# Identity products that go on into the second batch of a linear-attention and three-gate maxout kernel

## The chip, the cores and the metric

One core of one Trainium2 chip runs the whole problem. The metric is the device time of one execution in microseconds (us). Four engines compute: TensorE (PE in the rows; PEld is its weight load), VectorE (DVE), ScalarE (ACT) and GpSimd (POOL). SyncE's queue (SPq) issues the DMAs.

## The reference

There are 8 batches of 8 heads, 576 positions and a head dimension of 64. The attention's output, 4608 tokens of 512 features, goes through a layer of three gates and one output matrix.

```python
q_s = exp(q - max(q, -1)); q_s = q_s / (sum(q_s, -1) + 1e-09)
k_s = exp(k - max(k, axis=2)); k_s = k_s / (sum(k_s, axis=2) + 1e-09)
kv = einsum('bhsd,bhse->bhde', k_s, v)
x = einsum('bhsd,bhde->bhse', q_s, kv)        # as rows of 512
h = maximum(maximum(x @ w1, x @ w2), x @ w3)  # 512 to 768
return h @ w_out                              # 768 to 512
```

## The kernel before

The program is written out in full: no loop runs on the chip. Work is cut into steps, and a planner in the kernel's own Python (`Streams`) puts the steps of each engine in order. It keeps one clock for each engine (`self.clock["T"]` is TensorE's), adds a cost for each step, and issues next the step that may begin first. The costs only decide the order; on the chip, semaphores decide when something runs. What the planner thinks idle and what is idle on the chip are therefore two things.

Heads are taken in pairs, four pairs to a batch. A pair of batch 0 or 1 goes through these lines. `kt` is exponentiated (L692, ACT) and turned by four transposes into a `pa` bank (L698) and a fifth into the small bank (L699). ACT or DVE copies both to `ke` (L703 from `pa`, L704 from the small bank). The product of keys and values goes into the small bank (L773, 20 rows on PE), and ACT scales it into `bdf` (L783). The queries are turned (L899) and copied to `qf` (L903, ACT or DVE). L941 multiplies `qf` by `bdf`; ACT takes the high word of the result (L944), for some pairs PE subtracts it (L947), and ACT or DVE takes the low word (L949 or L952). The gates (L1052) multiply these words by the words of the weights `wa`, three products to a step, twelve to a gate. Slices of the weights are loaded and split at the same time (L546, L555 to L584).

The small bank is one PSUM bank of 512 columns, of which a pair has columns 128 to 255 for L699 and L704, 256 to 383 for L773 and L783; one pair (pair 1) has columns 384 to 511 for sums. Columns 0 to 127 are used by nothing. Batch 0 takes its small banks from the pool `pf` of four. Batch 1 (pairs 4 to 7) takes them from the pool `sm`, which has one bank, so that pair after pair has the same bank.

Before batch 1 takes it, that bank belongs to a tile `spare`. Into it go products of the identity with itself (L509), 128 columns of float32, each of which is two MATMUL rows in the trace; nothing reads them. `Streams.issue` calls `fill` with the hole that the planner sees ahead of a TensorE step, as long as TensorE's planned clock is under `SPARE[2]`:

```python
if e == "T" and SPARE[0] < t and self.clock["T"] < SPARE[2]:
    self.fill(max(self.clock["T"], SPARE[0]), t)
```

`fill` gives 0.65 of the hole to products of 0.225 us each, and writes them ahead of the step. By `self.taken.get("sm")` it stops once a pair of batch 1 has the bank.

Tiles are handed out by pools, and the framework writes the semaphores. It orders the accesses of different engines to one PSUM bank as whole accesses to that bank, whatever their columns: an access waits for those that stand ahead of it in the order of the program.

Of the kernel before, what the change touches and what calls it, by code (L numbers as in the profile page):

```python
# [8 lines left out]
F32 = mybir.dt.float32  # L9
# [22 lines left out]

COLD = 11.5, 1.85

SPARE = 4.4, 11.5, 42.0, 0.65

FIRST, CHUNK, SLICE = 144.74, 26.23, 2.59

# [160 lines left out]
class Streams:  # L199
# [100 lines left out]
    def fill(self, a, b):  # L300

        n = int((min(b, SPARE[1]) - a) / (0.225 * COLD[1])) if a < SPARE[1] else 0
        a = max(a, SPARE[1])
        n += int((b - a) * SPARE[3] / 0.225) if b > a else 0
        if n > 0 and not self.taken.get("sm"):
            self.spare(n)

    def issue(self, t, e, c, s):
        step = s[4]
        if e == "T" and t < COLD[0]:  # L310
            c *= COLD[1]
        if e == "T" and SPARE[0] < t and self.clock["T"] < SPARE[2]:
            self.fill(max(self.clock["T"], SPARE[0]), t)
        end = t + c
# [26 lines left out]
def linear_attention_then_maxout_ffn(  # L341
# [27 lines left out]
    nc = tc.nc  # L369
    B, H, S, D = 8, 8, 576, 64  # L370
    DM, DF = 512, 768
    P = 128
# [4 lines left out]
    CH = 512  # L377
# [40 lines left out]
    sm = ctx.enter_context(tc.tile_pool(name="sm", bufs=BANKS[1], space=PSUM))  # L418
    dram = ctx.enter_context(tc.tile_pool(name="dram", bufs=1, space=bass.MemoryType.DRAM))
    start_stack = ExitStack()  # L420
    start = start_stack.enter_context(tc.tile_pool(name="start", bufs=2, side="right"))
# [28 lines left out]
    ident = const.tile([P, P], F32, name="ident")  # L450
# [29 lines left out]
    for i in range(0, P, BL):  # L480
        nc.vector.tensor_scalar(
            out=ident[i : i + BL, :], in0=count[i : i + BL, :], scalar1=turned_count[i : i + BL, i : i + 1],
# [19 lines left out]
    for c in range(PAIRED, B + 1, 2):  # L502
        in_pf += [("S", c, i) for i in range(4)] + [(c, "y", t) for t in range(8)]
    st = Streams({"pf": 4, "pa": BANKS[0], "sm": BANKS[1], "hp": NJ, "tmp": 3, "ke": 2, "kep": 1, "qe": 2, "qf": 1, "qt": 1, "tb": 1, "qT": 1, "qhl": 1, "xr": 1, "ws": len(ws), "hs": 3}, {"pf": in_pf, "hs": in_hs, "ws": in_ws, "tb": list(range(TURNED * NP, B * NP, 2))})
    spare = sm.tile([P, CH], F32, name="sm")

    def products_for_nothing(n):
        for i in range(n):
            nc.tensor.matmul(out=spare[:, 0:P], lhsT=ident, rhs=ident, start=True, stop=True)  # L509

    st.spare = products_for_nothing
    turn_pools = []
# [91 lines left out]
    class Pair:  # L604
# [30 lines left out]

        def take_small(self):
            self.sm = (pf if self.b == 0 else sm).tile([P, CH], F32, name="pf" if self.b == 0 else "sm")

        def k_load(self):
            if self.b:  # L640
                prev = self.ago("ksub") if self.n >= NP + 2 else None
                if self.turned:
                    yield Step("S", 0.5, [prev], gives=("k", self.n), kb=(128, 2304))
                    nc.sync.dma_start(out=self.kt, in_=k_cols[self.b, self.g])
                elif self.m == 0:
                    yield Step("S", 0.5, [prev, ("ksub", self.n - 1)], gives=("k", self.n), kb=(128, 5120))
                    nc.sync.dma_start(
                        out=kboth.rearrange("p h s d -> p (h s d)"), in_=k_rows[self.b - TURNED, self.g // 2]
                    )
# [923 lines left out]
```

## Time and profile before

| | us |
|---|---|
| three runs | 645.25, 645.35, 646.13 |
| their median | 645.35 |
| the profiled execution | 646.05 |
| its span, first to last instruction | 644.2 |
| PE busy within the span | 629.7 |

The profiled execution is 1.85 us longer than its span, and 0.70 us longer than the median of the runs. Its mean granted TensorE clock is 0.997 of full speed.

### The profile page before, as it was taken

The page shows a single profiled execution, that of the slowest core. Times are in us where ns is not written, and L with a number is a line of the kernel's source. Part 1 is how long each engine was busy: PE and PEld are TensorE (multiplying, and loading weights), DVE is VectorE, ACT ScalarE, POOL GpSimd, SP SyncE. Part 2 cuts the span into 40 slices and gives each one's busy share as a digit, 9 for nine tenths or more (in the row PEclk, how much of TensorE's full clock was granted, in tenths as well). Part 3 has the DMA queues.
Part 4 walks back from the last instruction along what each step waited for, and adds up shares of the span by engine and source line. Part 5 has one row for each costly group of instructions (what it writes and reads, how often), then busy time and mean ns, then how long its engine had stood idle before and what let it go on. Part 6 is the DMA issues. An engine that isn't in the chain of part 4 may idle for free.

```text
span 644.2 us, 9789 instructions
## 1 busy us (share of the span) xinstructions
PE 629.7 (98%) x3460; PEld 506.7 (79%) x3460; DVE 423.1 (66%) x750; ACT 309.7 (48%) x678; POOL 58.0 (9%) x57
## 2 busy tenths in 40 slices
PE   6889999999999999999999999999999999999997
PEld 5757877888777787777877877888887888888886
DVE  8988986498997988988666889342425812243420
ACT  5998374235565655855453674322223622213131
POOL 1343333110010000010010000000000000000000
PEclk9999999999999999999999999999999999999999
DMA  8976476798767568999889534576663136666122
GB/s 330 394 246 253 153 229 242 260 342 270 233 222 268 193 206 249 338 293 351 261 279 301 161 117 139 170 240 192 193 191 114 57 127 195 193 195 195 36 65 66
DMA packets 89169, 137.88 MB, mean 214 GB/s; under 512 B 7200, under 2 KB 54816, under 8 KB 86432
## 3 DMA queue, kind: packets, MB, share of 16 engines
q1 hardware_dynamic: 89040, 137.12, 64.8%
q8 instruction: 28, 0.46, 0.3%
q10 hardware_dynamic: 80, 0.13, 0.1%
q14 instruction: 21, 0.17, 0.1%
HBM read 97.12 MB, written 33.03 MB: 202 GB/s over the span
## 4 chain that ended last, share of the span: by engine, by line
PE 74%; DVE 10%; DMA 9%; ACT 3%; issue 1%; SPq 1%; DVEq 0%; ACTq 0%
PE pf L1276 37%; PE pf L1099 18%; PE pf L1052 14%; DMA wst<-in_w_dram 3%; DMA kt<-in_k_rows_dram 2%; DMA bdf<-keep_w 2%; DVE tb L870 1%; PE pa L746 1%; DVE xb L1209 1%; PE pa L969 1%; DMA qT<-tb 1%; DVE bdf L1165 1%; DMA qt<-in_q_rows_dram 1%; DVE xf L1213 1%; DVE mix L1171 1%
## 5 line engine op out<-in xcount | busy, mean ns | idle before, releaser
L1276 PE MATMUL pf<-xb,ws 128*128 128x512 f32 x1134 | 260.8, 390 | 0.2 <-DVE mm L1305 0.2
L1276 PEld LDWEIGHTS pf<-xb,ws 128*128 128x128 f32 x1134 | 212.0, 188 | 45.3 <-DVE mm L1305 0.7
L1052 PE MATMUL pf<-x,wa 128*128 128x512 f32 x648 | 158.6, 399 | 1.0 <-ACT x L949 0.8
L1052 PEld LDWEIGHTS pf<-x,wa 128*128 128x128 f32 x648 | 120.4, 189 | 30.3 <-issue 1.9
L1305 DVE TENSOR_TENSOR mm<-pf,mm 128x512 f32<-128x512 f32 x36 | 24.8, 690 | 88.7 <-PE pf L1276 88.5
L1099 PE MATMUL pf<-oh,hs 128*128 128x512 f32 x192 | 59.4, 390 | 0.0
L1324 ACT COPY pf<-pf 128x512 f32<-128x512 f32 x27 | 15.4, 572 | 84.5 <-PE pf L1276 84.5
L857 ACT ACTIVATE qt<-qt,qs 128x64 f32<-128x64 f32 x171 | 43.4, 336 | 8.7 <-DVE qs L851 6.2
L1099 PEld LDWEIGHTS pf<-oh,hs 128*128 128x128 f32 x192 | 36.0, 188 | 7.7
L570 POOL TENSOR_TENSOR wx<-wx,wst 128x512 int32<-128x512 int32 x24 | 36.0, 1526 | 62.4 <-issue 22.2
L1118 ACT COPY m<-pf 128x512 f32<-128x512 f32 x31 | 18.1, 585 | 44.4 <-PE pf L1099 30.9
L716 POOL PARTITION_ALL_REDUCE kma<-km x24 | 18.5, 773 | 215.4 <-DVE km L713 165.8
L1099 PE MATMUL pf<-ol,hs 128*128 128x512 f32 x96 | 37.7, 393 | 0.0
L870 DVE STREAM_TRANSPOSE tb<-qt 128x576 f32<-128x576 f32 x24 | 30.2, 1272 | 3.3 <-DMA qT<-tb 2.2
L1317 ACT COPY u<-pf 128x512 f32<-128x512 f32 x27 | 15.8, 586 | 32.0 <-PE pf L1276 32.0
L1099 PE MATMUL pf<-oh,mix 128*128 128x512 f32 x96 | 30.2, 395 | 0.0
L1064 DVE TENSOR_TENSOR m<-pf,m 128x512 f32<-128x512 f32 x36 | 24.6, 683 | 8.0 <-PE pf L1052 8.0
L1099 PE MATMUL pf<-ol,h_h 128*128 128x512 f32 x72 | 28.5, 395 | 0.0
L1099 PE MATMUL pf<-oh,h_l 128*128 128x512 f32 x72 | 28.1, 390 | 0.0
L1099 PE MATMUL pf<-oh,h_h 128*128 128x512 f32 x72 | 28.0, 389 | 0.0
L1364 DVE TENSOR_TENSOR hs<-mm,hs 128x512 fp32r<-128x512 f32 (+1 forms) x32 | 16.9, 552 | 13.5 <-ACT hs L1362 13.5
L1317 ACT COPY s<-pf 128x512 f32<-128x512 f32 x27 | 15.8, 587 | 19.4 <-PE pf L1276 16.8
(165 smaller groups left out, 837.5 us busy)
## 6 DMA issues: line engine op xcount, KB each, us to landing
ws<-keep_s SPq DMA_DIRECT2D x108, 256.0 KB, 3.1
ws<-keep_a SPq DMA_DIRECT2D x81, 256.0 KB, 3.1
wst<-in_w_dram SPq DMA_DIRECT2D x12, 1024.0 KB, 7.8
keep_a<-wa SPq DMA_DIRECT2D x12, 768.0 KB, 6.8
keep_s<-mix SPq DMA_DIRECT2D x9, 1024.0 KB, 6.1
vt<-in_v_rows_dram SPq DMA_DIRECT2D x24, 325.0 KB, 4.8
kt<-in_k_rows_dram SPq DMA_DIRECT2D x12, 640.0 KB, 6.4
qt<-in_q_rows_dram SPq DMA_DIRECT2D x12, 576.0 KB, 4.7
```

The source lines that it names most:

```text
L570: nc.gpsimd.tensor_add(out=x.bitcast(I32)[:, at], in0=x.bitcast(I32)[:, at], in1=low.bitcast(I32)[:, at])
L716: nc.gpsimd.partition_all_reduce(kma, km, P, bass_isa.ReduceOp.max)
L857: nc.scalar.activation(out=rows3[:, s, :], in_=rows3[:, s, :], func=AF.Copy, scale=qs[:, s : s + 1])
L870: nc.vector.transpose(out=tb[:, self.m].rearrange("p e (c s) -> p s e c", s=QS), in_=self.qt.rearrange("p s (e c) -> p s e c", e=2),)
L1052: nc.tensor.matmul(out=ps, lhsT=l[:, cc, js], rhs=r, start=(cc == 0 and t == 0), stop=(cc == NC - 1 and t == 2))
L1064: nc.vector.tensor_max(out=m, in0=self.m.pop((j, i)), in1=m)
L1099: nc.tensor.matmul(out=po, lhsT=l, rhs=r[:, j, :], start=(j == 0 and i == 0), stop=(j == NJ - 1 and i == 2))
L1118: nc.scalar.copy(out=o, in_=po)
L1276: nc.tensor.matmul(out=bank[on], lhsT=w[:, k, a], rhs=x[:, b, k], start=(i == 0 and p in ("P1", "P5")), stop=(i == 5), skip_group_check=True,)
L1305: nc.vector.tensor_max(out=m, in0=bank[on], in1=m)
L1317: nc.scalar.copy(out=f, in_=bank[on])
L1364: nc.vector.tensor_tensor(out=o[:, 1, jj], in0=mm[:, h, jj, ts], in1=o[:, 0, jj].bitcast(F32), op=ALU.subtract)
```

## The change

The bound on TensorE's planned clock goes from 42 to 100; the test that stopped at batch 1 goes; products are counted with 0.35 added ahead of the rounding down; and the products go to the small bank that was taken last, in its columns 0 to 127. No step moves, and no step is added to the plan.

```diff
-SPARE = 4.4, 11.5, 42.0, 0.65
+SPARE = 4.4, 11.5, 100.0, 0.65
...
-        n += int((b - a) * SPARE[3] / 0.225) if b > a else 0
-        if n > 0 and not self.taken.get("sm"):
+        n += int((b - a) * SPARE[3] / 0.225 + 0.35) if b > a else 0
+        if n > 0:
             self.spare(n)
...
-    spare = sm.tile([P, CH], F32, name="sm")
+    spares = [sm.tile([P, CH], F32, name="sm")]
 
     def products_for_nothing(n):
         for i in range(n):
-            nc.tensor.matmul(out=spare[:, 0:P], lhsT=ident, rhs=ident, start=True, stop=True)
+            nc.tensor.matmul(out=spares[0][:, 0:P], lhsT=ident, rhs=ident, start=True, stop=True)
...
             self.sm = (pf if self.b == 0 else sm).tile([P, CH], F32, name="pf" if self.b == 0 else "sm")
+            if self.b:
+                spares[0] = self.sm
```

## Rows read from the trace of the kernel before

**Rows 1.** TensorE by stage: length, busy time (instructions), granted clock, DMA share, GB/s

```profile
0.00:42.00 42.00, 34.10 (x272) 1.00 0.88 328
...
50.00:93.00 43.00, 43.00 (x225) 1.00 0.58 202
...
250.00:400.00 150.00, 149.77 (x875) 1.00 0.79 250
```

**Rows 2.** The same view, single microseconds from 46 to 51

```profile
46.00:47.00 1.00, 1.00 (x21) 0.97 0.79 262
47.00:48.00 1.00, 1.00 (x3) 0.50 0.89 328
...
50.00:51.00 1.00, 1.00 (x3) 0.82 1.15 420
```

**Rows 3.** All instructions of line L509: duration ns min/median/max, first and last start

```profile
L509 PE MATMUL sm<-ident x68: 273/275/580, 5.5 to 30.0; 128*128 128x128 f32 x68
```

**Rows 4.** Timeline of TensorE, 15 to 20: start, length, instructions [idle before, releaser]

```profile
15.07 2.72 PE L509 MATMUL sm<-ident 128*128 128x128 f32 x22
18.98 0.66 PE L698 MATMUL pa<-ident,k 128*128 128x128 f32 x4 [1.19 <-ACT k L692]
```

**Rows 5.** Timeline of TensorE, 32 to 58

```profile
32.97 0.97 PE L1052 MATMUL pf<-x,wa 128*128 128x512 f32 x3
33.87 0.95 PE L773 MATMUL sm<-vt,ke 128*64 128x64 f32 x20
...
35.08 0.85 PE L1052 MATMUL pf<-x,wa 128*128 128x512 f32 x3
35.77 0.60 PE L899 MATMUL pa<-ident,qe 128*128 128x128 f32 x4
36.13 5.32 PE L1052 MATMUL pf<-x,wa 128*128 128x512 f32 x21
41.28 1.02 PE L941 MATMUL pa<-qf,bdf 128*128 128x512 f32 x2
42.14 0.60 PE L698 MATMUL pa<-ident,kt 128*128 128x128 f32 x4
43.53 0.30 PE L699 MATMUL sm<-ident,kt 128*64 128x128 f32 x1 [0.79 <-ACT bdf L783]
44.14 0.50 PE L947 MATMUL pa<-x,minus 128*128 128x512 f32 x1 [0.31 <-ACT x L944]
44.48 0.60 PE L899 MATMUL pa<-ident,qe 128*128 128x128 f32 x4
45.94 0.95 PE L773 MATMUL sm<-vt,ke 128*64 128x64 f32 x20 [0.86 <-ACT ke L704]
46.81 3.05 PE L1052 MATMUL pf<-x,wa 128*128 128x512 f32 x6
...
51.93 5.74 PE L1052 MATMUL pf<-x,wa 128*128 128x512 f32 x24
```

**Rows 6.** Timeline of ScalarE, 33 to 48

```profile
33.43 0.26 ACT L704 COPY ke<-sm 64x128 f32<-64x128 f32 x1
...
35.98 0.57 ACT L949 CAST x<-pa 128x512 fp32r<-128x512 f32 x1
...
42.85 0.63 ACT L783 ACTIVATE bdf<-sm,rk 64x64 f32<-64x64 f32 x2
...
45.63 0.26 ACT L704 COPY ke<-sm 64x128 f32<-64x128 f32 x1
...
46.73 0.58 ACT L949 CAST x<-pa 128x512 fp32r<-128x512 f32 x1
```

**Rows 7.** Timeline of all engines, 80 to 105

```profile
82.77 0.59 ACT L1061 COPY m<-pf 128x512 f32<-128x512 f32 x1 [0.98 <-PE pf L1052]
...
103.56 1.66 PE L1052 MATMUL pf<-x,wa 128*128 128x512 f32 x6 [0.77 <-ACT x L949]
```

**Rows 8.** Timeline of DVE, 44 to 83

```profile
57.71 0.69 DVE L1064 TENSOR_TENSOR m<-pf,m 128x512 f32<-128x512 f32 x1 [1.11 <-PE pf L1052]
```

## The prediction

> **What bounds the kernel now.** I read TensorE's busy time by stage first, because the page has PE at 98% of the span. From 50 us on it has no hole worth naming: 43.00 of 43 up to 93, 149.77 of 150 from 250 to 400 [rows 1]. So a microsecond by which TensorE reaches the stage at 50 earlier or later is one at the end, provided that what feeds it moves too. The one hole further on is 0.77 at 103.56, behind an ACT copy. I followed that back through the chain of waits: a weight slice's landing, its issue behind POOL's work, DVE and ACT work, and at 82.77 an ACT copy that waited for a gate on PE [rows 7]. That chain hangs on TensorE too, and moves with it.
>
> Second, the granted clock. It is 1.00 up to 42 and from 51 on [rows 1, 2]. From about 46.94 to 50.36 (0.97, then three microseconds at 0.50, then 0.82) it is at 0.50, that is at 1.2 instead of 2.4 GHz [rows 2]. These are 0.06 + 3.00 + 0.36 = 3.42 us in which PE is busy throughout, so 1.71 us of TensorE's time are lost. Before the fall PE stood idle for 0.79, 0.31 and 0.86 us between 42.7 and 45.94, with little but transposes between [rows 5]. This is what the change can win.
>
> Third, PE beside ACT from 32 to 52. Up to 42.7 PE runs nearly without idle time; then it waits for L783, L944 and L704, all of ACT [rows 5]. ACT is busy without a pause there, so what delays one ACT instruction delays those behind it.
>
> **How many products, and where.** The count is read from the code: the planner's clock, worked through with the listed costs, gives the holes. By the old formula they give 34 products, and the trace has 68 rows of two to a product [rows 3], so the reading is right. In the old stretch the added 0.35 changes no count. New are, ahead of these steps in PE's order: S1, one ahead of the gate at 32.97; S2, two ahead of L773 at 33.87; S3, three ahead of the gate at 35.08; S4, two ahead of L698 at 42.14; S5, one ahead of L947 at 44.14; S6, two ahead of L899 at 44.48; S7, one ahead of L773 at 45.94; S8, two ahead of the second gate step in the run at 46.81; S9, one ahead of L773 of pair 7 [rows 5]. That is 15 products. L509 should show 98 rows.
>
> **The price of one.** 22 rows took 2.72, the last of them 0.275, so a row starts every 2.445/21 = 0.116 us [rows 3, 4]; a product is 0.23, fifteen are 3.5. In holes they are free, elsewhere they are time. S1 to S3 stand where PE has no hole on the chip.
>
> **The added wait.** The trace shows none: the old products went to a bank without any reader. Bounds: nothing, if only columns count; or, if a bank counts whole, the end of the ACT read that stands ahead of the product in the program. I take the second, since the framework orders accesses by bank. S1 then waits for L704 of pair 4 (ends 33.69), S4 for L783 of pair 4 (ends 43.48), S6 for L704 of pair 5 (ends 45.89) [rows 6]; S2, S3, S5, S7, S8 and S9 find their readers done. Behind a waiting product stands all of PE's queue. The other way round, L704 and L783 of pair 5 also wait for the products ahead of them in their bank, but these are over by then.
>
> The trace has no row on this, so a page may be weighed: the Trainium skill (PSUM — Partial Sum Buffer, PSUM bank collisions raise a hardware error) asks that accesses be kept apart by bank and quadrant and not by address. No run here shows it yet. By it the sum below holds (+0.2); by address it would be that of the third rival (-1.4).
>
> **The walk, with the clock kept.** S1 starts at 33.69 + 0.05 = 33.74 in place of the gate's 32.97, and ends at 33.97. The gate's three products take 0.69 (35.08 to 35.77): 34.66. S2 takes 0.46: L773 starts at 35.12, 1.25 late. L773 and L947 take 33.87 to 35.08 = 1.21: 36.33. S3 takes 0.69: 37.02. Gate and L899 take 35.08 to 36.13 = 1.05: 38.07, which is 1.94 late. The run of 21 that follows had to wait for L949: at 0.23 a product (24 in 5.74, the last 0.39 long) it needs 4.83 of its 5.15, so 0.32 is won back. It ends at 42.90, L941 after 0.86 at 43.76; L698 stood there at 42.14 [rows 5].
>
> ACT's part: L949 waits for L947, which starts at 35.12 + 0.87 = 35.99 and lasts 0.50. So L949 starts at about 36.50, 0.52 late, and all of ACT behind it [rows 6]. L783 ends at 44.00 for 43.48, L704 of pair 5 at 46.41 for 45.89.
>
> S4 waits for L783: 44.05 to 44.51. Five transposes at 0.11: 45.06. S5: 45.29. L947 (44.14 to 44.48, 0.34): 45.63. S6 waits for L704: 46.46 to 46.92. L899 (0.36): 47.28. S7: 47.51. L773 (0.87): 48.38, where the gates began at 46.81. S8 and six products of 0.23: 48.84 and 50.22. L941 0.86, three products 0.69 and L899 0.36: 52.13, where 51.93 stood [rows 5]. So TensorE reaches its long stage **0.2 us late**: it is 1.57 late at the gates of 46.81 and pays S8's 0.46, and wins back 1.71 by the clock and a little by L949 (46.73 to 47.31), which the old run had to wait for and the new one finds ready.
>
> Next late is DVE: L903 of pair 4 waits for the L899 that moved from 44.48 to 46.92, and holds DVE's queue for about a microsecond. That reaches the splitting of the next slices; but DVE stands idle for 1.11 at 57.7, waiting for PE [rows 8], and makes it up there. I put it at nothing, at 1 if that cover comes too late. S9 costs 0.23 on PE, which the wait of 0.77 ahead of 103.56 takes up [rows 7]: nothing, or 0.23 without it. The changed owner of the bank adds no wait, since the next pair's first writer is PE itself, behind the products in its own queue.
>
> The sum is +0.2 against the profiled 646.05: 646.25. That execution lies 0.70 above the median of the runs, 645.35, whose terms are the same: 645.55, said as **645.5**. About 0.2% (1.3 us) is what a measurement of this kernel tells from no change.
>
> **The rivals.** *The clock falls all the same.* S1 to S9 as walked, but PE still idles ahead of S1, 0.29 ahead of S4 and 0.83 ahead of S6, with transposes between. For it: the three old pauses were no longer than these. Against it: 1.19 us of idle time after 22 rows of these products, with transposes behind it, left the clock at 1.00 [rows 1, 4]. It decides at the beginning of the run that stood at 46.81. Then 1.71 is not won back: +1.9, 647.25 in the runs' terms, 0.3% slower.
>
> *The clock did not fall in the median run.* The profile is 0.70 above it, and one of three runs as slow as the profile. Without the fall the old run would reach 50.42 for 51.93 (L773's end at 46.81, one product, the wait for L949 to 47.36, five products to 48.51, then L941, three products, L899). The change then only costs: 52.13 against 50.42, +1.7, or 647.0. Against it: the runs lie 0.88 apart, not 1.5.
>
> *Only columns count.* Then no product waits for ACT. S1 delays the gate of 32.97 by 0.23 at the most, and by the same steps S4 ends by 43.45 and S7 by 45.62; L773 waits for L704 to 45.94 as before, so all that stands ahead of it is free. S8 fills the wait for L949 but for 0.14, and the run of 24 starts at 50.56: -1.4, 644.0. If the products cost nothing at all it is 50.42, -1.5: the most that the change can give in this stretch. Against it: the order by bank.
>
> *Late work on DVE reaches a gate.* +1 or more on top of the forecast, 646.5. Against it: the pause of 1.11 [rows 8].
>
> **Chances.** The forecast (within 1 us of 645.5) 0.49; clock falls 0.25; median without the fall 0.09; only columns count 0.11; late DVE 0.06. Within 0.2% of before: the forecast, the late DVE for the most part and a third of the columns, which end on the bound, 0.57 with small parts of the slow ones. Faster: 0.10. Slower: 0.33. The range takes in the clock's fall above and the case of columns below, 644.2 to 647.4; the forecast's own is 644.8 to 646.3.
>
> **What would show it.** 98 rows of L509, 30 of them after 33 us. S1, S4 and S6 released by ACT (L704, L783, L704), with idle time ahead of them; L773 of pair 4 near 35.1 and of pair 5 near 47.5; L949 half a microsecond later; the granted clock at 1.00 from 46 to 51; the run of 24 near 52.1. If the products start at once behind the PE instruction ahead of them, the bank does not count whole and the time is near 644. If 0.50 still stands somewhere between 44 and 54, the clock rival holds. The prediction is wrong if the end moves otherwise than the run of 24 does, that is if something off TensorE sets the pace from 52 to 104, or if PE's dense stages are not as tight as their busy time says.

## The result and the profile after

The changed kernel takes 650.08 us (median of 22 runs, 647.23 to 654.13) against 646.34 of the kernel before (22 runs, 644.39 to 652.52): ratio 1.0054, 95% interval 1.0036 to 1.0072. It is 0.5% slower, and 650.08 lies outside the predicted range. Three executions that took 702, 1617 and 3496 us, two of the kernel before and one of a version of the change, are left out of the counts and medians of the experiments below.

The profiled execution after took 648.66 us with a span of 646.9. First TensorE's stages, as in [rows 1, 2] (stretch, length, busy time and instructions, granted clock, DMA share, GB/s):

```profile
0.00:42.00 42.00, 32.59 (x274) 1.00 0.87 316
...
46.00:47.00 1.00, 0.71 (x6) 1.00 1.02 328
47.00:48.00 1.00, 0.59 (x5) 1.00 0.69 213
48.00:49.00 1.00, 1.00 (x18) 1.00 0.85 303
...
50.00:51.00 1.00, 1.00 (x7) 1.00 0.85 258
...
93.00:104.00 11.00, 11.00 (x48) 1.00 0.98 339
...
173.00:250.00 77.00, 76.74 (x512) 1.00 0.75 243
250.00:400.00 150.00, 148.88 (x869) 1.00 0.80 249
```

The clock stays at 1.00 where it had been at 0.50 [rows 2]. The stage from 250 to 400, full to 0.23 us before, now has 1.12 us of idle time.

All instructions of the identity products, against [rows 3]:

```profile
L509 PE MATMUL sm<-ident x98: 270/275/579, 5.5 to 90.6; 128*128 128x128 f32 x98
```

These are 30 rows more, 15 products. TensorE's timeline after, against [rows 5] (start, length, instructions, idle time before and its releaser; lines behind 638 have moved by two):

```profile
30.88 0.66 PE L700 MATMUL pa<-ident,kt 128*128 128x128 f32 x4
...
34.46 0.49 PE L509 MATMUL sm<-ident 128*128 128x128 f32 x2 [0.76 <-ACT ke L706]
...
36.01 0.95 PE L775 MATMUL sm<-vt,ke 128*64 128x64 f32 x20
...
38.95 5.04 PE L1054 MATMUL pf<-x,wa 128*128 128x512 f32 x21
43.82 1.02 PE L943 MATMUL pa<-qf,bdf 128*128 128x512 f32 x2
44.99 0.71 PE L509 MATMUL sm<-ident 128*128 128x128 f32 x4
...
47.41 0.71 PE L509 MATMUL sm<-ident 128*128 128x128 f32 x4 [0.70 <-ACT ke L706]
...
48.71 0.95 PE L775 MATMUL sm<-vt,ke 128*64 128x64 f32 x20
49.58 0.71 PE L509 MATMUL sm<-ident 128*128 128x128 f32 x4
...
53.44 1.87 PE L1054 MATMUL pf<-x,wa 128*128 128x512 f32 x7
...
90.47 0.38 PE L509 MATMUL sm<-ident 128*128 128x128 f32 x2
90.79 0.95 PE L775 MATMUL sm<-vt,ke 128*64 128x64 f32 x20
...
110.87 0.39 PE L1101 MATMUL pf<-ol,h_h 128*128 128x512 f32 x1
```

ScalarE ahead of S4 and ahead of S6, from the timeline of that engine:

```profile
44.32 0.62 ACT L785 ACTIVATE bdf<-sm,rk 64x64 f32<-64x64 f32 x2
...
47.09 0.26 ACT L706 COPY ke<-sm 64x128 f32<-64x128 f32 x1
```

S1 to S7 and S9 stand where the prediction put them; S8 stands ahead of all six gate products of its run, as the prediction's walk has it, and not ahead of the second step. From here on three marks cut the span, since executions start unequally: the first transposes of pair 4 (30.88 here), the first output product (110.87 here), and the first product with `ws` (L1276 before, 269.78 here). **Path** is the time from the first mark to the second, **middle** from the second to the third, **rest** from the second to the end. Here they are 79.99, 158.91 and 536.0.

### The profile page after: what moved, and what is told of

It is laid out like the page before. It is cut to its first block, busy times and chain, and to the rows that moved or that the text cites. A ratio compares the mean times of both kernels' runs of the same rounds, so it can differ in the third digit from the quotient of the medians.

```text
span 646.9 us, 9844 instructions
## 1 busy us (share of the span) xinstructions
PE 631.6 (98%) x3490; PEld 508.9 (79%) x3490; DVE 422.6 (65%) x750; ACT 309.4 (48%) x678; POOL 57.9 (9%) x57
## 4 chain that ended last, share of the span: by engine, by line
PE 75%; DVE 10%; DMA 9%; ACT 3%; SPq 2%; issue 1%; POOL 1%; DVEq 0%; ACTq 0%; POOLq 0%
PE pf L1278 37%; PE pf L1101 18%; PE pf L1054 14%; DMA qT<-tb 2%; DVE tb L872 2%; PE pa L748 1%; DMA keep_w<-wx 1%; DMA bdf<-keep_w 1%; PE pa L971 1%; DMA kt<-in_k_rows_dram 1%; SPq L889 1%; DVE xb L1211 1%; DMA q<-in_q_first_dram 1%; DMA qt<-in_q_rows_dram 1%; DVE bdf L1167 1%
## 5 line engine op out<-in xcount | busy, mean ns | idle before, releaser
L1054 PE MATMUL pf<-x,wa 128*128 128x512 f32 x648 | 156.6, 396 | 0.2 <-ACT bdf L785 0.2
```

The source lines that it names most:

```text
L1054: nc.tensor.matmul(out=ps, lhsT=l[:, cc, js], rhs=r, start=(cc == 0 and t == 0), stop=(cc == NC - 1 and t == 2))
```

## The experiments

**Both kernels once more.** No edit.

> The kernel before, unchanged, to see how much of the difference between the two traces is there without any change. In the first trace of before, the first product of L1099 stands at 110.28 us and the end comes 533.9 us later; in the trace of after 110.87 and 536.0. Downstream theory (the two traces differ by chance from 222 us on, in the stage that DMAs and DVE bound): this trace again shows another length from L1099 to the end, anywhere from 533 to 537. Theory of the products (what they do ahead of 110 us is carried on): 533.9 within 0.5. Ratio to the kernel before 1.000 within 0.002 in both.

> The changed kernel, unchanged, for a second trace. Theory of the products: slower by some 0.5% again, L1099 about 0.1 us ahead of before's in terms of the first turned keys, and the rest of 2 us lost between 222 and 365 us as in the first trace (536.0 from L1099 to the end). Downstream theory: the same ratio, but the places where TensorE stops after 110 us are others than in the first trace, and the length from L1099 to the end differs from 536.0 by more than 1 us.

Measured: before again 645.36 (12 runs), ratio 0.9994 [0.9966, 1.0022]; after again 649.93 (12 runs), 1.0062 [1.0039, 1.0085]. Ratios are to runs of the kernel before from the same series; there are three series, each with its own. The profiled execution of before again did not have the clock's fall. TensorE's timeline there:

```profile
30.41 0.66 PE L698 MATMUL pa<-ident,kt 128*128 128x128 f32 x4
...
43.77 0.30 PE L699 MATMUL sm<-ident,kt 128*64 128x128 f32 x1 [0.77 <-ACT bdf L783]
44.38 0.50 PE L947 MATMUL pa<-x,minus 128*128 128x512 f32 x1 [0.31 <-ACT x L944]
...
46.18 0.95 PE L773 MATMUL sm<-vt,ke 128*64 128x64 f32 x20 [0.86 <-ACT ke L704]
...
50.80 4.38 PE L1052 MATMUL pf<-x,wa 128*128 128x512 f32 x18
...
108.06 0.39 PE L1099 MATMUL pf<-ol,h_h 128*128 128x512 f32 x1
```

And its stages of one microsecond, columns as above:

```profile
46.00:47.00 1.00, 0.82 (x20) 1.00 0.86 307
47.00:48.00 1.00, 0.94 (x7) 1.00 1.02 360
48.00:49.00 1.00, 1.00 (x6) 1.00 0.91 367
```

The same three pauses, 0.77, 0.31 and 0.86, and the clock stays at 1.00. So the fall is not fixed by the program. Each run lists its mean granted clock: the three profiles with a fall in this document list 0.997, the ten without one 0.999 or 1.000. Of the 33 runs of before in this series 17 have 0.999 or 1.000 (no fall), with a median of 644.54; 16 have less, with 647.04. Of the changed kernel's runs 17 of 22 had no fall (649.84), and in this series all 12 (649.93). The change does hold the clock in most runs, and with the clock held on both sides it costs 649.93 - 644.54 = 5.4 us, where the medians of all runs of the series differ by 4.0 (645.93 before).

It is lost in two places. The path is 110.87 - 30.88 = 79.99 and, after again, 80.47, against 108.06 - 30.41 = 77.66 without the fall: 2.3 to 2.8 more. The rest is 536.0 and 537.88 against 534.50 and, in the first profile of before, 533.97: 1.5 to 3.9 more, in a stretch that the change does not touch. Neither expectation came out whole: the rest moved by 0.5 between the two traces of before and by 1.9 between those of after, but in both of after PE waits at the same three lines. What ended PE's waits of after again from 110 to 300 (line, releaser: us in total, times, longest):

```profile
PE pa L971 <- DVE bd L758: 1.4, 1, 1.4
PE pf L1101 <- DVE h_l L1073: 1.2, 1, 1.2
PE pf L1278 <- DVE mm L1307: 0.4, 1, 0.4
```

**Which groups cost.** The same edit with other numbers: groups 2, 3, 5, 7, 8, 9 (10 products), 4 to 9 (9 products, twice), 1 to 3 (6 products).

```diff
+        self.held = 0
...
+        if n > 0 and self.taken.get("sm"):
+            self.held += 1
+            n = n if self.held in (2, 3, 5, 7, 8, 9) else 0
         if n > 0:
             self.spare(n)
```

> S1, S4 and S6 (5 of 15 products) are left out: the products that wait for a copy of ACT. The rest, S2, S3, S5, S7, S8 and S9, stays. If the waits cost the time: the ratio falls from about 1.005 to 1.000 within 0.002, the run of 24 gate products at most 0.5 us from its place in before in terms of the first turned keys. If the added work as such costs it: about two thirds of the loss stays, 1.003. Downstream theory: 1.005 as long as anything is moved.

> S1 to S3 (6 of 15 products) are left out: those that stand where TensorE has no hole on the chip. S4 to S9 stay, S4 and S6 with their waits. If filling the place without holes costs the time: faster than before by up to 1.4 us, 0.998 to 1.000, with the clock at 1.00 through 42 to 52. If the waits of S4 and S6 cost it: 1.003 to 1.005. Downstream theory: 1.005 as long as anything is moved.

> The changed kernel without its first three groups (6 of the 15 products), again. Direct cost: the groups at 42 to 48 us hold 9 products, of which 4 wait for ScalarE; the run of 24 products begins 1.2 to 1.6 us later than in a run of before with the clock held, if the clock holds here too. Theory of the instruction packets: 9 products move the blocks some 2.5 us ahead of the work; rest of the span between 534.3 and 537. Theory of lateness: rest over 534.3 in proportion to the lateness, about 535.5. Ratio by both 1.002 to 1.004.

> The changed kernel with its first three groups alone (6 of the 15 products, ahead of 36 us). Direct cost: the run of 21 products begins some 1.3 to 2 us later, of which the wait for the block-diagonal matrix near 43 us takes back most; by it the run of 24 begins within 0.5 us of before. Nothing fills the pauses at 43 to 47 us, so the clock should fall in some of the runs as it does in the kernel before; if it is held nearly always, it is the early groups that hold it. Theory of the instruction packets: 24 more instructions, rest 534 to 536. Ratio 1.000 to 1.002.

Measured: without S1, S4 and S6 647.08, 1.0029 [1.0001, 1.0056], path 78.41. S4 to S9 alone 646.95 (11 runs), 1.0028 [1.0003, 1.0053], the second time 647.25, 1.0021 [0.9996, 1.0046], path 79.50. S1 to S3 alone 647.75, 1.0018 [0.9996, 1.0040]; there the clock fell in 5 of 12 runs, the profiled one among them, and the run of 24 began 22.96 us after the first mark, 1.2 later than in the first trace of before (21.77), where at most 0.5 was expected. PE by single microseconds in that profile:

```profile
46.00:47.00 1.00, 0.07 (x1) 1.00 0.95 262
...
48.00:49.00 1.00, 1.00 (x6) 0.67 0.86 336
49.00:50.00 1.00, 1.00 (x3) 0.50 0.94 350
```

S4 to S9 had a fall in 4 of 23 runs. That points to the groups at 42 to 48 us as those that hold the clock, though 5 of 12 against 4 of 23 is too few to show it. The three groups that wait are five products, 1.2 us by 0.23 each; leaving them out shortens the path by 1.6 to 2.1, products and waits together. What remains, ten products, costs 0.75 on the path. One of them waits too: what ended PE's waits from 30 to 50 without S1, S4 and S6 (S7 here stands ahead of the wait of 0.86 that was L773's):

```profile
PE sm L513 <- ACT ke L710: 0.9, 1, 0.9
```

**Instructions without a place in batch 1.** Two theories were left for the rest: that TensorE comes late to it, or that the length of TensorE's program matters. The queues in the profile after:

```profile
q1 hardware_dynamic: 89040, 137.12, 65.3%
q8 instruction: 28, 0.46, 0.3%
```

q8 brings instructions: 28 packets of 0.46 MB in all, 16 KB each, of which the trace has one about every 20 us; 0.3% of 16 engines' span of 646.9 us is some 31 us, so a packet takes about 1.1 us of one DMA engine. By their number they are TensorE's: 3490 matmul rows and as many weight loads over 28 packets are some 250 to a packet. A product is four instructions (two rows, two weight loads), so 64 products are about one packet and 15 a quarter of one. Therefore products of a column of ones with itself were put ahead of everything, where TensorE has nothing to do until 5.54; nothing reads them, and no group of batch 1 moves. The numbers tried: 15 and 32 on the kernel before; 49 and 17 on the changed one, which makes 64 and 32 with its own 15.

```diff
+    for i in range(15):
+        nc.tensor.matmul(out=spare[0:1, 0:1], lhsT=ones, rhs=ones, start=True, stop=True)
     st.spare = products_for_nothing
```

> The kernel before with 15 products of one column of ones with itself (one number each) ahead of everything on TensorE, which has nothing to do before 5.5 us: as many instructions in TensorE's stream as the change adds, without a place in batch 1. They are left unused. Theory of the instruction packets: TensorE's program comes in blocks of 16 KB over the DMA engines, about one every 20 us, and 15 products move every later block about 4 us ahead of the work; in the stage after the first output product those packets then meet other transfers. By it the path from the first transposes of pair 4 to the first output product stays at 77.7 us (80.1 where the clock falls), the rest of the span grows from 534.0-534.5 to 536-538 us, and the time is 1.003 to 1.005 of before. Theory of lateness: the rest of the span is longer only because TensorE comes late to it; by it nothing changes: rest 534.0-534.5, ratio 1.000 within 0.002.

> The kernel before with 15 products of ones ahead of everything, a second time, since 5 runs with the clock held are few. Theory of the instruction packets: rest of the span 536 to 537 us, first late product near 222 us at the transposes of the turned heads, ratio 1.002. Theory of lateness, or of chance in the transfers: rest 534 to 534.5, ratio 1.000.

> The kernel before with 32 such products of ones ahead of everything on TensorE, half a block of 16 KB: every later block comes some 10 us of work earlier. Theory of the instruction packets: the packets lie at other places of the stage again, the rest of the span differs from 534.0-534.5 by something between nothing and 3.5 us, and the place of the first late transfer is not that of the changed kernel. Theory of lateness: 534.0-534.5, ratio 1.000 within 0.002.

> The changed kernel with 49 such products of ones ahead of everything on TensorE: with the change's 15 they are 64, or 256 instructions, one whole block of 16 KB, so that the later blocks fall on the work as they did before. Theory of the instruction packets: the path up to the first output product stays long (80.0 to 80.5 us from the first transposes of pair 4), the rest of the span comes back from 536.0-537.9 to about 534.3, and the ratio to before is 1.002 to 1.003. Theory of lateness: rest 536-538, ratio 1.006 as the changed kernel has.

> The changed kernel with 17 products of ones ahead of everything: with its 15 they are 32, half a block, the number that left the kernel before without a late product after the first output product. Theory of the instruction packets: first output product 80.0 to 80.5 us after the first transposes of pair 4, rest near 534, ratio 1.002 to 1.003. Theory of lateness: rest 536 to 538, ratio 1.006.

> The changed kernel without the three groups that wait for ScalarE, which leaves 10 products, and with 22 products of ones ahead of everything, 32 in all. If the direct cost is the waits and the packets cost the rest, this keeps what holds the clock and pays 0.8 us up to the first output product and nothing after it: rest near 534, ratio 0.999 to 1.001. Theory of lateness: as without the 22, ratio 1.003.

Measured: 15 on before 647.17, 1.0021 [1.0001, 1.0041], again 647.43, 1.0032 [1.0011, 1.0053]; 32 on before 645.81, 1.0007 [0.9986, 1.0028]; 49 on the changed kernel 648.28, 1.0023 [1.0000, 1.0045]; 17 on it 647.39, 1.0024 [1.0006, 1.0042]; 22 on the one without S1, S4, S6 646.25, 1.0000 [0.9978, 1.0022]. The marks of all profiles:

```
products in    kernel                 clock   path    middle   rest
front+batch 1
 0 +  0        before                 fell    80.12   157.38   533.97
 0 +  0        before again           held    77.66   157.62   534.50
15 +  0        before, 15             held    77.97   159.67   536.94
15 +  0        before, 15 again       fell    80.41   158.39   535.59
32 +  0        before, 32             held    77.66   157.38   533.82
 0 +  6        S1 to S3               fell    81.19   157.61   534.13
 0 +  9        S4 to S9, second       held    79.50   158.27   536.05
 0 + 10        without S1, S4, S6     held    78.41   158.40   535.23
22 + 10        the same, 22           held    78.64   157.38   533.98
 0 + 15        after                  held    79.99   158.91   536.00
 0 + 15        after again            held    80.47   160.54   537.88
17 + 15        after, 17              held    80.10   157.38   535.23
49 + 15        after, 49              held    80.27   158.93   536.36
```

Fifteen products where they take no time leave the path at 77.97 and lengthen the rest by 2.4; in the second trace, which has the fall as the first trace of before has it, by 1.6 (535.59 against 533.97). In the first of them PE then waits at the same lines as after again:

```profile
PE pa L971 <- DVE bd L758: 1.1, 1, 1.1
PE pf L1278 <- DMA ws<-keep_s: 0.9, 1, 0.9
PE pf L1101 <- DVE h_l L1073: 0.7, 1, 0.7
```

With 32 in front PE of the kernel before has no wait at all there:

```profile
173.00:250.00 77.00, 77.00 (x513) 1.00 0.73 238
250.00:300.00 50.00, 50.00 (x275) 1.00 0.96 308
```

And the changed kernel, as late as ever at the first output product (80.10), has a middle as short as any, 157.38, once its products are 32. S1 to S3 alone, the latest of all (81.19), have a rest of 534.13, and the kernel before with the fall, as late as the changed one (80.12), has 533.97. Lateness is refuted.

What the transfers do there: the DMA view of the kernel before with 15 in front, 221 to 230 us (queue and kind, packets, MB, share of the 16 engines; then loads, KB each, median us to landing):

```profile
q8 instruction: 1, 0.02, 1.0%
...
kt<-in_k_rows_dram SPq DMA_DIRECT2D x1, 640.0 KB, 9.2
bdf<-keep_w SPq DMA_DIRECT2D x1, 512.0 KB, 6.6
```

The same view with 32 in front:

```profile
q1 hardware_dynamic: 958, 2.78, 97.9%
...
kt<-in_k_rows_dram SPq DMA_DIRECT2D x1, 640.0 KB, 7.5
bdf<-keep_w SPq DMA_DIRECT2D x1, 512.0 KB, 5.9
```

Both keep the 16 DMA engines busy for some 95% or more. In the first an instruction packet lies within the stretch, in the second none of q8. The landing of that key load in all profiles, and the q8 packets around it, in us after the first output product:

```
                         key load lands   q8 packets start
before, 32               120.7            104.7   123.9
after, 17                120.9            104.9   124.4
without S1 S4 S6, 22     121.4            104.8   123.8
after                    122.6             91.3   113.7
before                   122.9            100.3   120.5
S1 to S3                 123.1             96.9   113.8
before, 15 again         123.3             91.9   113.7
before again             123.4            100.9   119.3
without S1 S4 S6         123.4             95.1   114.8
S4 to S9, second         123.7             98.0   114.5
before, 15               124.2             91.4   115.0
after, 49                124.7            102.3   122.3
after again              124.8             91.2   115.3
```

The three kernels with 32 products have no packet between 105 and 123.8, and their key load lands by 121.4; the ten with a packet in between have it at 122.6 or later. The landing alone does not sort the kernels, though: in after it comes at 122.6 and the middle is 158.91, in before at 122.9 and the middle is 157.38.

What a packet does beside SyncE's issues can be read from that queue's timeline. Here are two rows of before, then one of after, then one of before with 15 in front (start, length):

```profile
222.97 0.42 SPq L1159 DMA_DIRECT2D bdf<-keep_w  x1
223.48 0.87 SPq L647 DMA_DIRECT2D kt<-in_k_rows_dram  x1
...
224.57 2.23 SPq L1161 DMA_DIRECT2D bdf<-keep_w  x1
...
223.39 2.38 SPq L649 DMA_DIRECT2D kt<-in_k_rows_dram  x1
```

In after the issue of `bdf` takes 2.23 for 0.42 us, and the packet at 113.7 in the table starts together with it; with 15 in front the issue of `kt` takes 2.38 for 0.87, beside the packet at 115.0. Behind the first output product the thirteen traces have 18 SyncE issues that took over 1 us more than the median of the same issue; all 18 overlap a packet of q8, which only 258 of the 5148 issues there do. So a held-up issue goes with a packet, and what SyncE issues next comes later; but it does not always cost: S1 to S3 alone has one of 2.81 us at 113.7 and a rest of 534.13.

Where the changed kernel's 15 products put the packets differs from the kernel before by up to 12 us (91.3 for 100.3, 172.7 for 184.4).

One result does not fit. With 64 products, one whole packet, the packets should lie as before, and up to 83 they do (22.7, 43.9, 61.3, 83.1 for 21.9, 43.6, 61.3, 82.4); then they come 2 to 3 us later (102.3, 122.3, 141.4 for 100.3, 120.5, 138.3). The rest stayed at 536.36 in the profile, not 534.3, though the runs with the clock held came down from 5.4 over those of before (649.93 against 644.54) to 3.3 (648.28 against 644.97). So the number of instructions moves the end, and 32 takes the middle's loss away; which transfer must meet a packet for a wait on PE to follow isn't settled.

## Why the prediction was wrong

**Right.** Fifteen products and 98 rows. The order by whole banks: S1 and S6 stand behind ACT's L706 with 0.76 and 0.70 us, S4 starts 0.05 after L785 ends (44.94). The Trainium skill (PSUM — Partial Sum Buffer, PSUM bank collisions raise a hardware error) asks for that guard; by address there would have been no such waits. The clock at 1.00 from 46 to 51. And the walk, in us from the first transposes of pair 4 (30.16 in the trace walked from, 30.88 after):

```
              predicted   measured
S1             3.58        3.58
L773, pair 4   4.96        5.13
run of 21      7.91        8.07
S4            13.89       14.11
S6            16.30       16.53
L773, pair 5  17.35       17.83
run of 24     21.97       22.56
```

It is 0.6 short in all, the largest part of it at S6, L899 and S7, which took 1.30 for 1.05 us. Against an execution with the fall (path 80.12 and, with 15 in front, 80.41) the path after, 79.99 to 80.47, is level within 0.5, as the forecast of +0.2 had it, though not in the way of the forecast: at the run of 24 it is 0.8 late (22.56 against 21.77), and gets that back as the wait of 0.77 ahead of 103.56 is gone. The late work on DVE cost nothing up to the first output product: against before with the clock held, after and after again lose 2.2 and 2.4 up to the run of 24 and only 0.2 and 0.4 behind it, about S9.

**Wrong, first step: "whose terms are the same: 645.55".** The fall of the clock was in the profiled execution and not in the median run: 64 of the 115 runs of before in the three series, 56%, had none (17 of 33, 8 of 12, 19 of 35, 20 of 35). They are 2.3 to 2.9 us faster than those with it (644.54, 644.44, 644.97 and 645.23 against 647.04, 647.30, 647.41 and 647.50). So in most runs there was no fall for the change to win back. This was the second rival, with a chance of 0.09, argued away by three runs that lay 0.88 apart. Its mechanism was right; its price, +1.7, was small against 2.2 at the run of 24 (22.56 for 20.40) and 2.3 to 2.8 at the first output product.

The fall's own worth was mis-sized as well, 1.71. At the run of 24 it is 21.77 - 20.40 = 1.37, but on the path 80.12 - 77.66 = 2.46, since the wait of 0.77 ahead of 103.56 [rows 7] belongs to it: the three profiles with a fall have one of 0.61 to 1.05 there, those without have none. S9 was to be free in that wait; with the clock held nothing covers it, and it takes 90.79 - 90.47 = 0.32.

**Wrong, second step: that TensorE's lateness at 50 "is one at the end".** The rest was taken as rigid because PE's dense stages have no hole [rows 1]; the prediction named this as a way for it to be wrong. The rest grew by 1.5 to 3.9 us, not by lateness, but with the number of TensorE's instructions: 15 idle products at the start do it to the kernel before (runs with the clock held 646.05 for 644.97, 646.73 for 645.23), and 17 more undo most of it in the changed one (647.38 against 645.23 of before, +2.2, where its path alone is 2.4 longer; its profile still has 0.7 us of waits behind 285). No step of the prediction priced an instruction other than by its time on its engine.

**The sum.** With the clock held on both sides the change costs 2.3 to 2.8 on the path and about as much behind it, 5.4 together. The median of all runs of before lies 1.4 above that of its runs without a fall (645.93 against 644.54), so against all runs 4.0 of it is left; the first comparison measured 3.7 (650.08 - 646.34).

**No version beats the kernel before.** Without the waiting groups, and with 32 products in all, the change pays 1.0 on the path (78.64), nothing behind it, and keeps the clock in 11 of 12 runs: 1.0000 [0.9978, 1.0022]. What the clock gives and what the products cost then cancel, within the 0.2% that is measured. Which of the products at 44 to 48 us hold the clock alone, and whether fewer would do, was not tried.

## What to carry to other kernels

One profile shows one execution: before a stall or a fall of the clock in it is booked as a gain, look whether the median run has it, by the granted clock of each run or by a second trace. A filler instruction is not free where its engine is idle if it shares a bank with readers: here it waited 0.70 and 0.76 us for a copy of other columns. It need not be free even where nothing waits for it: here the program's own instructions come over DMA engines that a later stage keeps busy, and 15 more products of no use moved the end. So an edit that adds or drops instructions should be judged beside a control that changes the count alone, at a place without other work; otherwise its cost and the shift of the packets can't be told apart.

## What the runs showed of the hardware

- Adding 15 products to a program of 3460 matmul rows moves later instruction packets by up to 11 us against the work, and makes the run 0.2 to 0.3% longer (1.0021 and 1.0032); adding 32 leaves the time as it was (1.0007).
- An issue on SyncE's queue can take 1 to 2 us longer beside a packet of TensorE's instructions (2.23 for 0.42 and 2.38 for 0.87 us); all 18 issues that were over 1 us longer than usual behind the first output product overlap such a packet.
- The clock's fall is not a function of the program: with pauses of 0.79, 0.31, 0.86 us it came (0.50 from 47), with 0.77, 0.31, 0.86 it did not. With the change it is rarer (5 of 34 runs of the changed kernel list a clock below 0.999, and none of the 24 with 49 or 17 products in front, against 51 of 115 of before), not impossible.
